# Attention and two mixture-of-experts layers on one core: the order of all instructions searched anew, with a tighter rule for taking operations and GpSimd's durations read from the trace

## The chip, the cores and the metric

The kernel runs on one core of one Trainium2 chip. The time is the device time of one execution in microseconds (us), the median over the runs of a kernel. The engines are called PE (TensorE, matrix multiplication), ACT (ScalarE), DVE (VectorE), POOL (GpSimd) and SP (SyncE, which here does nothing but issue DMAs). Each engine works through its own instructions strictly in the order in which the program lists them, and waits for the other engines by semaphores.

## The reference

Three layers for 4 batches, each with a sequence of 576 positions:

```python
# 1: attention, 8 heads of 64; 32 global positions see all, 512 local ones see the
#    global ones and a window of 32 to either side
s_g = scale * np.matmul(q_g, k_all.transpose(0, 1, 3, 2))
out_g = np.matmul(sm(s_g), v_all)
s_l = np.concatenate([s_lg, np.where(mask, s_ll, -1e9)], axis=-1)
out_l = np.matmul(sm(s_l), np.concatenate([v_g, v_l], axis=2))
# 2: causal attention by 4 experts, two of them taken for each position
logits = x @ w_gate
for e in range(E):
    q = x @ wq[e]; k = x @ wk[e]; v = x @ wv[e]
    ye = softmax(causal(scale * (q @ k.transpose(0, 2, 1)))) @ v @ wo[e]
    out += gate[e] * ye
# 3: wide layer with a convolution over 3 positions and a gate
h = np.maximum(x @ w_in, 0.0)
conv_out = sum(conv_w[k] * hp[:, k:k + S, :] for k in range(3))
out = h * (1.0 / (1.0 + np.exp(-conv_out))) @ w_out
```

## The kernel before, in words

**Stages.** For each batch b there are three stages. Stage A (`stage_a`, with `local` and `glob`) is layer 1: two halves u of the heads, each with two pairs of heads z. A pair's local scores (`scoresA`, L575 and L583) go to a tile of two PSUM banks; DVE takes the maxima (L586), POOL scales them (L372 on `st`), ACT makes eight exponentials (L592), PE transposes them in two groups of four (L599), ACT copies the transposes out of PSUM (L601), PE multiplies with the values (`pvA`, L612), DVE divides by the sums (L619 to L621), PE transposes the result (L629), and ACT and DVE split it into a high and a low part (L631, L378). The global rows of both pairs of a half take the same way in one piece (L648, L652, L654 and L656, L665, L667, then `pvG`, L675, and L679 to L699). Stage B (`stage_b`, `tiles`, `last`) is layer 2: projections (L727 for queries and keys, L747 for values and the gate), scores by query tiles (L811), a softmax whose exponentials are normalised on POOL (`nrmB`, L830), transposes (L838), products with the values (L857). The gate of a batch is a chain of small operations on DVE, POOL and ACT (L765 to L779). Stage C is layer 3: a product with `wo` and `w_in` multiplied beforehand (`h`, L940), the convolution (L372 on POOL, L955 on DVE), the gate (L959, L960), a split (L964, L378) and the product with `w_out` (`out`, L982), and a store (L998 and L1000, at the very end L989, L992 and L994). Matrices enter PE as a high and a low part, in three products each.

**Once only.** The weights `wqv` are loaded in four pieces and split (ACT L449, POOL L375). `wo` is loaded and split (ACT L495, DVE L378 on `wo`). `w_in` and `w_out` come in 8 pieces each and are decoded from 64-bit numbers (L477 to L487) and split; `w_in` is multiplied with `wo` (L514).

**What sets the order.** No order is written by hand. The functions record operations (`op`), each with an engine, a planned duration, and a priority; the class `Schedule` then lists all of them in one order by a planner that keeps a clock for each engine (`run`). A priority is a time on a line: the stage's begin and end from the table `PLAN`, a place inside it from `SUB`, and for each of the 1,906 operations a correction from the table `FINE`. At each step `run` looks at every engine's operations that are ready: those are allowed whose priority is at most `HORIZON` behind the least one that is still open; of the allowed ones that could begin within `SLACK` of the earliest, the one of least priority is taken, where for PE an operation in another tile mode than the last counts as `HOLD` later. Buffers (work tiles, PSUM banks, three `kq` tiles, four `v` tiles) are given out in the same pass; `CAPS` limits how many buffers of a kind may be held at a time. The loads of `kq`, `v` and the weights are operations of SP like all others, and each queue keeps the order of the list.

```python
            if o.prio > limit:
                continue
...
            c = min((c for c in cands if c[0] <= m + self.SLACK), key=rank)
```

PE's array works in several tile modes: whole (128x128: projections, `h`, `out`, all transposes), 64x32 (L575, L583, L648), 128x32 (L612, L675, L901), 64x128 (L811), 128x64 (L857). Ahead of all, nine matmuls with no use for the result keep PE busy until the first inputs are there (L1024).

Of the kernel before, what the change touches and what calls it, by code (L numbers as in the profile page):

```python
# [8 lines left out]
F32 = mybir.dt.float32  # L9
# [5 lines left out]
ALU = mybir.AluOpType  # L15
# [7 lines left out]
LEAST = 2.0 ** -15  # L23
MOST = 2.0 ** 125
# [121 lines left out]
class Schedule:  # L146
# [4 lines left out]
    SLACK = 0.092  # L151
    HOLD = 0.538
    HORIZON = 3714.57
# [153 lines left out]
def t_act(n, psum=False, ptr=0):  # L307
    return (167 + 0.83 * n + (0 if psum else 33) + 93 * ptr) * 1e-3


def t_dve(n, stt=False):
    return (150 + 1.04 * n + (70 if stt else 0)) * 1e-3


def t_pool(n, two=False):
    return (200 + (2.1 if two else 1.05) * n) * 1e-3


PLAN = {"A": [(-119.1, -47.3), (-21.7, 63.1), (38.1, 315.4), (307.0, 360.9)],
        "B": [(-137.7, -21.3), (148.2, 259.2), (249.9, 388.0), (376.3, 509.9)],  # L320
        "C": [(148.2, 401.7), (371.1, 480.9), (486.2, 654.7), (-670.0, 740.1)],
        "F": (162.2, -63.1),
        "U": (116.3, 210.9),
        "W": (-56.5, -20.9)}


CAPS = dict(raw=1, t=36, p=62, P=37, PT=2, PU=33, hb=44, cv=110, Pg=117, PGT=84)

MEM = (14, 11, 3, 4, 4)

SUB = {"lk": -1.365, "lv": -20.969, "ly": -0.281, "lw": -129.791, "ag": 0.056, "az": 0.113, "bq": -0.039, "bp": 0.366, "bv0": -1.297,
       "bv": 0.609, "bg": 2.203, "b0": -0.896, "b1": 1.269, "b2": 1.01, "b3": 1.37, "bl": 1.25, "bs": 0.036, "ch": 0.098,
       "co": 0.775, "cm": 0.686, "cf": -0.537, "cz": 0.902, "pi": 0.0, "pu": 0.0}


@with_exitstack
def body(ctx, tc, kq, vA, wqv, woT, w_in, conv_w, w_out, cmask, out, trace=None,
         tune=None):
    nc = tc.nc
    NB = kq.shape[0]  # L340
    pe, act, dve, pool, sp = nc.tensor, nc.scalar, nc.vector, nc.gpsimd, nc.sync

    sb = ctx.enter_context(tc.tile_pool(name="sb", bufs=1))
    ps = ctx.enter_context(tc.tile_pool(name="ps", bufs=1, space=PSUM))
# [20 lines left out]
    W = lambda n=1, keep=0, group=None: Buf(W_, n, keep, group)  # L365
# [3 lines left out]
    op = sch.op  # L369

    def scale_pool(dst, src, s):
        pool.tensor_scalar(dst, src, s, 1.0, op0=ALU.mult, op1=ALU.mult)  # L372
# [26 lines left out]
    vB = T([128, 5, 4, 65], F32, "vB")  # L399
# [55 lines left out]
    def decode(srcs, n, lead, tag, on_pool, spare=None):  # L455

        if spare:
            raw, t = Buf(D_, 1, 1), Buf(D_)
            p, tv, pv = (t, 1), (lambda: t.ap()[:, :512]), (lambda: t.ap()[:, 512:])
            dz = ["dz"]  # L460
# [635 lines left out]
```

## Time and profile before

| | before |
|---|---|
| median of 3 runs | 422.12 us (421.61 to 422.59) |
| the profiled execution, its own time | 423.22 us |
| its span, first to last instruction | 421.1 us |
| outside the span | 2.1 us |
| mean granted clock of PE | 0.986 |
| moved by DMA | 42.34 MB |

The span is what the profile shows in detail; the profiled execution is 1.1 us over the median of the runs. PE is busy nearly throughout, so the parts of the span that can shrink are those in which PE waits, those in which its clock is low, and what it loses between operations of different kinds.

### The profile page before, as it was taken

The page shows a single profiled execution, that of the slowest core. Times are in us where ns is not written, and L with a number is a line of the kernel's source. Part 1 is how long each engine was busy: PE and PEld are TensorE (multiplying, and loading weights), DVE is VectorE, ACT ScalarE, POOL GpSimd, SP SyncE. Part 2 cuts the span into 40 slices and gives each one's busy share as a digit, 9 for nine tenths or more (in the row PEclk, how much of TensorE's full clock was granted, in tenths as well). Part 3 has the DMA queues.
Part 4 walks back from the last instruction along what each step waited for, and adds up shares of the span by engine and source line. Part 5 has one row for each costly group of instructions (what it writes and reads, how often), then busy time and mean ns, then how long its engine had stood idle before and what let it go on. Part 6 is the DMA issues. An engine that isn't in the chain of part 4 may idle for free.

```text
span 421.1 us, 13314 instructions
## 1 busy us (share of the span) xinstructions
PE 402.0 (95%) x5605; PEld 362.5 (86%) x5605; DVE 281.5 (67%) x559; ACT 253.1 (60%) x616; POOL 172.7 (41%) x358
## 2 busy tenths in 40 slices
PE   7867899899899999999999999999999999999996
PEld 3656699677589999999889999899999999999996
DVE  2249858987787688886356558568675637758650
ACT  2866765765866746676476565675554556554531
POOL 3442563675775526460313232543331662262110
PEclk9888999999999999999999999999999999999999
DMA  8998922624523620233330200000000000000101
GB/s 309 396 345 299 339 98 75 215 90 147 184 82 107 207 97 2 89 125 125 120 127 0 94 5 2 28 29 2 2 2 2 26 28 29 29 0 28 54 26 54
DMA packets 15179, 42.34 MB, mean 101 GB/s; under 512 B 1552, under 2 KB 6416, under 8 KB 15120
## 3 DMA queue, kind: packets, MB, share of 16 engines
q1 hardware_dynamic: 15120, 41.49, 27.9%
q8 instruction: 44, 0.72, 0.7%
q14 instruction: 15, 0.12, 0.1%
HBM read 37.03 MB, written 4.46 MB: 99 GB/s over the span
## 4 chain that ended last, share of the span: by engine, by line
PE 84%; ACT 6%; DVE 4%; issue 3%; POOL 2%; DMA 1%; SPq 0%; ACTq 0%; DVEq 0%
PE acc L982 21%; PE acc L940 12%; PE acc L727 12%; PE acc L747 7%; PE acc L811 4%; PE acc L857 4%; PE acc L838 4%; PE acc L599 3%; PE acc L612 3%; PE acc L583 3%; ACT work L592 2%; PE acc L629 2%; DMA work<-in_w_out_dram 1%; PE acc L514 1%; PE acc L648 1%
## 5 line engine op out<-in xcount | busy, mean ns | idle before, releaser
L982 PE MATMUL acc<-xg,wuh 128*128 128x272 f32 x512 | 99.4, 292 | 0.0
L982 PEld LDWEIGHTS acc<-xg,wuh 128*128 128x128 f32 x512 | 79.9, 188 | 1.6 <-issue 1.2
L955 DVE SCALAR_TENSOR_TENSOR work<-work,cw 128x272 f32<-128x272 f32 x128 | 68.9, 560 | 18.2 <-POOL work L372 16.8
L982 PE MATMUL acc<-xg,wul 128*128 128x272 f32 x256 | 73.5, 287 | 0.0
L372 POOL TENSOR_SCALAR work<-work,cw 128x272 f32<-128x272 f32 x64 | 34.6, 551 | 53.3 <-ACT work L947 47.5
L940 PE MATMUL acc<-xg,wfh 128*128 128x274 f32 x256 | 51.6, 297 | 0.5 <-ACT work L667 0.5
L830 POOL TENSOR_SCALAR work<-work,st,gate 128x128 f32<-128x128 f32 (+3 forms) x64 | 46.5, 735 | 7.9 <-DVE st L827 6.1
L727 PE MATMUL acc<-xg,wqvh 128*128 128x272 f32 x256 | 49.7, 292 | 0.0
L982 PEld LDWEIGHTS acc<-xg,wul 128*128 128x128 f32 x256 | 48.2, 188 | 0.0
L592 ACT ACTIVATE work<-acc,st 128x128 f32<-128x128 f32 x128 | 37.1, 384 | 13.8 <-POOL st L372 13.7
L823 ACT ACTIVATE work<-acc,st 128x128 f32<-128x128 f32 (+3 forms) x64 | 33.1, 524 | 17.3 <-DVE st L816 12.0
L940 PEld LDWEIGHTS acc<-xg,wfh 128*128 128x128 f32 x256 | 40.2, 189 | 1.5 <-ACT work L667 0.8
L727 PEld LDWEIGHTS acc<-xg,wqvh 128*128 128x128 f32 x256 | 39.9, 188 | 0.9 <-issue 0.7
L940 PE MATMUL acc<-xg,wfl 128*128 128x274 f32 x128 | 37.1, 290 | 0.0
L727 PE MATMUL acc<-xg,wqvl 128*128 128x272 f32 x128 | 36.8, 287 | 0.0
L586 DVE TENSOR_REDUCE st<-acc 128x8 f32<-128x1024 f32 x16 | 19.5, 1219 | 22.6 <-PE acc L583 22.5
L947 ACT ACTIVATE work<-acc 128x546 f32<-128x546 f32 x32 | 20.0, 628 | 21.2 <-PE acc L940 17.6
L747 PE MATMUL acc<-wqvh,xg 128*128 128x260 f32 (+1 forms) x160 | 31.3, 286 | 0.0
L378 DVE TENSOR_TENSOR xg<-acc,xg 128x512 fp32r<-128x512 f32 (+3 forms) x56 | 22.6, 410 | 12.4 <-ACT xg L631 3.4
L840 ACT ACTIVATE work<-acc 128x512 f32<-128x512 f32 (+1 forms) x44 | 23.7, 558 | 11.3 <-PE acc L838 10.6
L378 DVE TENSOR_TENSOR xg<-work,xg 128x544 fp32r<-128x544 f32 x32 | 23.7, 744 | 9.4 <-ACT xg L964 8.6
L964 ACT ACTIVATE xg<-work 128x544 fp32r<-128x544 f32 x32 | 20.9, 659 | 13.8 <-DVE work L960 9.4
(138 smaller groups left out, 865.3 us busy)
## 6 DMA issues: line engine op xcount, KB each, us to landing
v<-in_vA_dram SPq DMA_DIRECT2D x32, 487.5 KB, 5.1
kq<-in_kq_dram SPq DMA_DIRECT2D x16, 624.0 KB, 5.2
work<-in_w_out_dram SPq DMA_DIRECT2D x8, 512.0 KB, 5.7
early<-in_w_in_dram SPq DMA_DIRECT2D x8, 512.0 KB, 6.8
out_dram<-work SPq DMA_DIRECT2D x15, 272.0 KB, 2.2
early<-in_wqv_dram SPq DMA_DIRECT2D x4, 386.0 KB, 8.8
early<-in_woT_dram SPq DMA_DIRECT2D x1, 512.0 KB, 9.0
out_dram<-work SPq DMA_DIRECT2D x2, 136.0 KB, 1.7
```

Source lines behind the costliest of these rows:

```text
L372: pool.tensor_scalar(dst, src, s, 1.0, op0=ALU.mult, op1=ALU.mult)
L378: dve.tensor_tensor(lo, src, hi.bitcast(F32), op=ALU.subtract)
L592: op("ACT", t_act(128, 1, 1), lambda y=y, t=t, sl=sl: act.activation(P[y].ap()[:, sl], S_(y)[:, sl], AF.Exp, bias=st.ap()[:, 8 + 4 * y + t ...
L727: pe.matmul(acc.ap()[:, 512 * z:512 * z + 272], wa[:, c, m], xa[:, s], start=(n == 0), stop=(n == 11))
L747: pe.matmul(acc.ap()[:r, :260], x[:, o_ + 128 * i:o_ + 128 * i + r], wa[:, c, :], start=(n == 0), stop=(n == 11))
L823: op("ACT", t_act(w, 1, 1) + .21, lambda tv=tv, st=st, y=y, k_=k_, Pb=Pb, c=c, h=h, w=w: act.activation(Pb.ap()[:, c:c + w], tv()[:, y, k_ ...
L830: op("POOL", t_pool(w), lambda Pb=Pb, st=st, c=c, h=h, e=e, w=w, i=i: pool.tensor_scalar(Pb.ap()[:, c:c + w], Pb.ap()[:, c:c + w], st.ap() ...
L840: op("ACT", t_act(128 * nb, 1), lambda PT=PT, tp=tp, nb=nb: act.activation(PT.ap()[:, :128 * nb], tp.ap()[:, :128 * nb], AF.Copy), r=[tp], ...
L940: pe.matmul(acc.ap()[:, 512 * f:512 * f + 274], a[:, p, sl], ov_(b)[:, x, p, 270 * z:270 * z + 274], start=(k == 0), stop=(k == 5))
L955: op("DVE", t_dve(272, 1), lambda hv=hv, cvv=cvv, f=f, F=F, z=z, k=k, o_=o_: dve.scalar_tensor_tensor(cvv()[:, f], hv()[:, f, o_:o_ + N], ...
L964: op("ACT", t_act(544), lambda G=G, cv=cv: act.activation(G.ap()[:, :544], cv.ap()[:, :544], AF.Copy), r=ct, w=[(G, 0)], tag="gh")
L982: pe.matmul(acc.ap()[:, 512 * m:512 * m + N], w[:, F, sl], G.ap()[:, o_ + N * f:o_ + N * f + N], start=(F == 0 and n == 0), stop=(F == 7 a ...
```

## The change

Only numbers change: three constants of the planner, the tables `FINE`, `PLAN`, `CAPS` and `SUB`, and the planned durations of some operations of POOL. The operations, their operands and the buffers' sizes stay. `HORIZON` falls from 3714.57 (no limit in practice) to 0.69, so that operations are taken nearly in the order of their priorities; `SLACK` is 0; `HOLD` is larger. `FINE` has other numbers throughout (its first entries are shown).

```diff
-    SLACK = 0.092
-    HOLD = 0.538
-    HORIZON = 3714.57
+    SLACK = 0.0
+    HOLD = 0.97
+    HORIZON = 0.69
...
-    FINE = {0: -42.4, 1: 62.9, 2: 79.2, 3: 48.2, 4: -51.1,
+    FINE = {0: -19.0, 1: 99.2, 2: 109.9, 3: 110.1, 4: 78.8,
...
-CAPS = dict(raw=1, t=36, p=62, P=37, PT=2, PU=33, hb=44, cv=110, Pg=117, PGT=84)
+CAPS = dict(raw=22, t=50, p=74, P=35, PT=13, PU=38, hb=19, cv=118, Pg=105, PGT=78)
...
-        op("POOL", 0.3, lambda: pool.memset(vB, 0.0), w=[("vB", i) for i in range(5)] + ["vBone", "vBraw"])
+        op("POOL", 1.2, lambda: pool.memset(vB, 0.0), w=[("vB", i) for i in range(5)] + ["vBone", "vBraw"])
...
-        op("POOL", t_pool(n), lambda: pool.tensor_scalar(a(F32), a(F32), MOST, LEAST, op0=ALU.min, op1=ALU.max), r=dz, w=[t], tag=tag)
+        op("POOL", t_pool(n) - .125, lambda: pool.tensor_scalar(a(F32), a(F32), MOST, LEAST, op0=ALU.min, op1=ALU.max), r=dz, w=[t], tag=tag)
...
-        op("POOL", .25, lambda: scale_pool(st.ap()[:, 8:16], st.ap()[:, 0:8], 0.125), r=[st], w=[(st, 1)], tag="sclA")
+        op("POOL", .205, lambda: scale_pool(st.ap()[:, 8:16], st.ap()[:, 0:8], 0.125), r=[st], w=[(st, 1)], tag="sclA")
...
-            op("POOL", .29, lambda i=i, r=r: pool.tensor_copy(lg[:r, i], vB[:r, i, :, 64]), r=[("vB", i)], w=[("lg", i)] + (["lg"] if i == 0 else []), tag="lg")
+            op("POOL", .19, lambda i=i, r=r: pool.tensor_copy(lg[:r, i], vB[:r, i, :, 64]), r=[("vB", i)], w=[("lg", i)] + (["lg"] if i == 0 else []), tag="lg")
...
-                    op("POOL", t_pool(w), lambda Pb=Pb, st=st, c=c, h=h, e=e, w=w, i=i: pool.tensor_scalar(
+                    op("POOL", .342 + .00084 * w, lambda Pb=Pb, st=st, c=c, h=h, e=e, w=w, i=i: pool.tensor_scalar(
```

The lists of instructions show what moves. PE, ACT, DVE, POOL and SP have the same operations as before; ACT and DVE have two instructions more each, because for one more half the small copies L699 and L378 fall into two pieces of 64x32. Counted over PE's list, the tile mode changes 124 times instead of 134; from the first projection (L747) on it is 108 instead of 113, and between whole-array products and transposes there are 90 changes instead of 86. Up to that first projection the list holds the same instructions of PE in both kernels, in another order. In the second half of the program the list is nearly the old one, block by block.

**PE, first half of the first batch.** L583 is the end of a `scoresA` (the third), the transposes of exponentials are L599, of the global ones L665, L612 is `pvA`, L675 `pvG`, L648 the global scores of the second half. Before:

```order
L583 MATMUL acc<-kq 32x128 x32
L599 MATMUL acc<-ident,work 128x128 x4
L675 MATMUL acc<-v,work 32x65 x20
L599 MATMUL acc<-ident,work 128x128 x4
L612 MATMUL acc<-v,work 32x65 x32
L684 MATMUL acc<-ident,work 128x128
L599 MATMUL acc<-ident,work 128x128 x8
L629 MATMUL acc<-ident,work 128x128 x4
L612 MATMUL acc<-v,work 32x65 x32
L648 MATMUL acc<-kq 32x480 x4
L648 MATMUL acc<-kq 32x64 x4
```

With the change:

```order
L583 MATMUL acc<-kq 32x128 x32
L599 MATMUL acc<-ident,work 128x128 x4
L665 MATMUL acc<-ident,work 128x128 x5
L599 MATMUL acc<-ident,work 128x128 x4
L612 MATMUL acc<-v,work 32x65 x32
L675 MATMUL acc<-v,work 32x65 x20
L599 MATMUL acc<-ident,work 128x128 x4
L648 MATMUL acc<-kq 32x480 x4
L648 MATMUL acc<-kq 32x64 x4
L684 MATMUL acc<-ident,work 128x128
L599 MATMUL acc<-ident,work 128x128 x8
L629 MATMUL acc<-ident,work 128x128 x4
```

All three first `scoresA` now stand ahead of the first transpose (before, transposes stood between them), the first `pvA` stands ahead of `pvG`, and the second half's global scores come before the second `pvA` and no longer behind it.

**SP, the first loads.** `kq` holds queries and keys of a pair of heads, `v` the values of one head (four of them per half), `wqv` and `woT` weights, `cmask` masks. Before:

```order
L427 DMA kq<-in_kq_dram 128x1248
L433 DMA cb<-in_cmask_dram 128x928
L427 DMA kq<-in_kq_dram 128x1248
L427 DMA v<-in_vA_dram 128x975
L427 DMA kq<-in_kq_dram 128x1248
L437 DMA cb<-in_cmask_dram 128x304
L427 DMA early<-in_wqv_dram 128x772
L427 DMA v<-in_vA_dram 128x975
L427 DMA early<-in_wqv_dram 128x772 x2
L427 DMA v<-in_vA_dram 128x975 x2
```

With the change:

```order
L433 DMA cb<-in_cmask_dram 128x928
L427 DMA kq<-in_kq_dram 128x1248 x2
L427 DMA early<-in_woT_dram 128x4x256
L427 DMA work<-in_conv_w_dram 128x48
L427 DMA kq<-in_kq_dram 128x1248
L427 DMA early<-in_wqv_dram 128x772
L427 DMA v<-in_vA_dram 128x975
L427 DMA early<-in_wqv_dram 128x772
L427 DMA v<-in_vA_dram 128x975
L427 DMA early<-in_wqv_dram 128x772
L427 DMA v<-in_vA_dram 128x975 x2
```

`woT` and the small `conv_w` are now ahead of all values; the small second piece of `cmask` has gone to a later place.

**POOL at the first gate.** The rows run from the first `epsB` (L826) to the scaling of the next batch's maxima (L372 on `st`); L767, L770 and L768 belong to the gate, L507 to the decoding of `w_in`. Before:

```order
L826 TENSOR_SCALAR st<-st 128x4
L767 TENSOR_TENSOR gw_84<-gw_84,cb 128x80
L770 TENSOR_TENSOR lg<-lg,gmx 128x20
L826 TENSOR_SCALAR st<-st 128x4
L768 TENSOR_TENSOR gw_83<-gw_83,gw_84 128x80
L372 TENSOR_SCALAR st<-st 128x8
```

With the change:

```order
L826 TENSOR_SCALAR st<-st 128x4
L767 TENSOR_TENSOR gw_84<-gw_84,cb 128x80
L770 TENSOR_TENSOR lg<-lg,gmx 128x20
L507 TENSOR_TENSOR early<-early,xg 128x512
L768 TENSOR_TENSOR gw_83<-gw_83,gw_84 128x80
L372 TENSOR_SCALAR st<-st 128x8
```

An L507 has come between L770 and L768, and the second L826 has gone behind the scaling.

## Rows read from the trace of the kernel before

**Rows 1.** The page: busy time, and PE, DVE, clock, DMA in 40 slices.

```profile
PE 402.0 (95%) x5605; PEld 362.5 (86%) x5605; DVE 281.5 (67%) x559; ACT 253.1 (60%) x616; POOL 172.7 (41%) x358
...
PEclk9888999999999999999999999999999999999999
DMA  8998922624523620233330200000000000000101
```

**Rows 2.** Busy time by stage: window, its length, PE, PEld, DVE, ACT, POOL, PEclk, DMA share, GB/s.

```profile
0.00:49.40 49.40, 36.88 (x893) 25.70 (x893) 26.61 (x52) 31.77 (x81) 20.45 (x39) 0.90 0.92 333
49.40:120.00 70.60, 67.62 (x1014) 56.60 (x1016) 56.22 (x119) 47.51 (x124) 41.89 (x71) 1.00 0.43 151
120.00:240.00 120.00, 120.00 (x1871) 111.68 (x1862) 83.53 (x160) 76.98 (x195) 50.04 (x102) 1.00 0.27 89
240.00:401.30 161.30, 160.93 (x1716) 152.23 (x1713) 109.76 (x220) 91.84 (x208) 58.82 (x146) 1.00 0.06 23
```

**Rows 3.** The chain that ended last, pieces between 18 and 50 us.

```profile
18.72 0.78 PE acc L675 x40
19.50 0.59 PE acc L599 x4
20.09 0.82 PE acc L612 x48
20.90 2.96 issue
23.86 0.66 PE acc L612 x16
...
34.39 1.64 issue
...
44.63 1.05 PE acc L648 x16
...
47.22 1.45 issue
```

**Rows 4.** Windows up to each of four stops of PE; the counts matter.

```profile
0.00:16.10 16.10, 12.83 (x223) 7.31 (x223) 3.49 (x4) 6.85 (x16) 5.48 (x17) 0.89 0.91 342
0.00:22.00 22.00, 16.52 (x350) 9.98 (x351) 5.39 (x8) 12.75 (x34) 8.52 (x21) 0.92 0.95 355
0.00:35.50 35.50, 25.72 (x606) 17.05 (x606) 14.02 (x27) 21.76 (x57) 13.57 (x30) 0.90 0.96 354
0.00:48.20 48.20, 36.14 (x859) 25.13 (x859) 26.23 (x51) 31.20 (x80) 19.38 (x37) 0.89 0.92 333
```

**Rows 5.** Timeline of PE, the first stop, and of SP, the third and fourth `v`.

```profile
16.19 0.67 PE L583 MATMUL acc<-kq 64*32 64x128 f32 x31 [0.24 <-issue]
...
7.59 1.56 SPq L427 DMA_DIRECT2D v<-in_vA_dram  x2
```

**Rows 6.** DMA issues between 8.5 and 9.3 us: the fourth `v`, us to landing.

```profile
v<-in_vA_dram SPq DMA_DIRECT2D x1, 487.5 KB, 9.1
```

**Rows 7.** Windows of ten us in the start.

```profile
10.00:20.00 10.00, 8.45 (x205) 6.14 (x205) 2.74 (x4) 8.46 (x26) 4.29 (x6) 0.83 1.05 398
30.00:40.00 10.00, 7.77 (x237) 6.26 (x225) 9.74 (x16) 6.25 (x18) 3.26 (x8) 0.88 0.94 367
40.00:50.00 10.00, 7.79 (x214) 5.75 (x214) 8.72 (x21) 8.03 (x20) 4.93 (x6) 0.95 0.82 252
```

**Rows 8.** Timeline of DVE between 24.5 and 31 us.

```profile
25.00 0.69 DVE L621 TENSOR_TENSOR work<-acc,st 128x512 f32<-128x512 f32 x1
...
25.80 1.21 DVE L378 TENSOR_TENSOR wo<-early,wo 128x1024 fp32r<-128x1024 f32 x1
27.04 0.30 DVE L378 TENSOR_TENSOR xg<-acc,xg 64x32 fp32r<-64x32 f32 x2
...
30.55 0.72 DVE L652 TENSOR_REDUCE st<-acc 128x1 f32<-128x544 f32 x1
```

**Rows 9.** The chain between 321 and 327 us.

```profile
321.00 0.92 PE acc L811 x12
321.91 1.70 PE acc L982 x12
323.61 1.52 PE acc L940 x12
325.13 1.49 PE acc L982 x12
```

**Rows 10.** The chain at the end of a wait for POOL, 269 us; two groups of POOL's instructions.

```profile
269.23 3.35 POOL work L830 x6
...
L830 POOL TENSOR_SCALAR work<-work,st,gate 128x128 f32<-128x128 f32 x16 | 10.4, 656 | 0.2
L507 POOL TENSOR_TENSOR early<-early,xg 128x512 f32<-128x512 f32 x8 | 10.8, 1345 | 8.3 <-DVE st L619 4.7 <-ACT xg L506 3.5
```

More of the change, by code (lines that the diff above doesn't have):

```diff
@@ L316, in t_pool @@
     return (200 + (2.1 if two else 1.05) * n) * 1e-3
[L319 to L324, printed above, removed]
-CAPS = dict(raw=1, t=36, p=62, P=37, PT=2, PU=33, hb=44, cv=110, Pg=117, PGT=84)
+PLAN = {"A": [(-119.7, -48.2), (-21.9, 62.9), (38.1, 315.6), (307.4, 361.3)],
+        "B": [(-137.7, -21.3), (148.5, 259.4), (249.8, 388.0), (376.1, 509.8)],
+        "C": [(148.5, 401.8), (371.4, 481.1), (486.1, 655.3), (-668.3, 746.0)],
+        "F": (162.3, -62.8),
+        "U": (116.1, 210.9),
+        "W": (-52.9, -24.7)}
+CAPS = dict(raw=22, t=50, p=74, P=35, PT=13, PU=38, hb=19, cv=118, Pg=105, PGT=78)
 MEM = (14, 11, 3, 4, 4)
-SUB = {"lk": -1.365, "lv": -20.969, "ly": -0.281, "lw": -129.791, "ag": 0.056, "az": 0.113, "bq": -0.039, "bp": 0.366, "bv0": -1.297,
-       "bv": 0.609, "bg": 2.203, "b0": -0.896, "b1": 1.269, "b2": 1.01, "b3": 1.37, "bl": 1.25, "bs": 0.036, "ch": 0.098,
-       "co": 0.775, "cm": 0.686, "cf": -0.537, "cz": 0.902, "pi": 0.0, "pu": 0.0}
+SUB = {"lk": 0.237, "lv": -18.39, "ly": -0.48, "lw": -130.134, "ag": 0.055, "az": 0.113, "bq": -0.04, "bp": 0.368, "bv0": -1.295,
+       "bv": 0.609, "bg": 2.204, "b0": -0.896, "b1": 0.535, "b2": 1.01, "b3": 1.37, "bl": 1.249, "bs": 0.036, "ch": 0.098,
+       "co": 0.775, "cm": 0.684, "cf": -0.537, "cz": 0.902, "pi": 0.0, "pu": 0.0}
 @with_exitstack
@@ L652, in glob @@
         op("DVE", t_dve(544), lambda: dve.tensor_reduce(st.ap()[:, 0:1], G.ap()[:, 32:576], axis=AX.X, op=ALU.max, negate=True), r=[G], w=[st], tag="maxG")
-        op("POOL", .25, lambda: scale_pool(st.ap()[:, 1:2], st.ap()[:, 0:1], 0.125), r=[st], w=[(st, 1)], tag="sclG")
+        op("POOL", .19, lambda: scale_pool(st.ap()[:, 1:2], st.ap()[:, 0:1], 0.125), r=[st], w=[(st, 1)], tag="sclG")
         op("ACT", t_act(480, 1, 1), lambda: act.activation(Pg.ap()[:, :640].rearrange("p (n c) -> p n c", n=5)[:, :, 32:128],
@@ L829, in tiles @@
                     Pb, c, h, e = Ps[n // per], w * (n % per), y * np_ + k_, 2 * p + y
-                    op("POOL", t_pool(w), lambda Pb=Pb, st=st, c=c, h=h, e=e, w=w, i=i: pool.tensor_scalar(Pb.ap()[:, c:c + w], Pb.ap()[:, c:c + w], st.ap()[:, 12 + h:13 + h], gate[:, i, e:e + 1],
+                    op("POOL", .342 + .00084 * w, lambda Pb=Pb, st=st, c=c, h=h, e=e, w=w, i=i: pool.tensor_scalar(Pb.ap()[:, c:c + w], Pb.ap()[:, c:c + w], st.ap()[:, 12 + h:13 + h], gate[:, i, e:e + 1],
                        op0=ALU.mult, op1=ALU.mult), r=[(st, 4), gt], w=[(Pb, n % per)], tag="nrmB")
```

2 lines of the change are left out of this document (1 added, 1 removed).

## The prediction

> **What bounds the kernel now.** I read the page's busy times first, then the windows by stage, then the chain of waits in the start, then single rows. PE is busy for 402.0 us and no other engine for over 281.5 [rows 1]; the reader should see in the slices that the clock is below full only in the first five, the same slices in which the DMA queues are full. The windows by stage say where the 19 us without PE lie [rows 2]: in the start, up to the first projection at 49.4 us, PE works 36.88 of 49.40 us, so 12.5 us are lost, at a mean clock of 0.90; from there to 120 us 3.0 us are lost; from 120 to 401.3 us only 0.4 us. The rest is the warm-up's begin and the tail after the last product. So from 120 us on a new order can win nothing by filling gaps, only by fewer changes of mode, and whatever gain there is must come from the start, with a little from the stretch behind it.
>
> In the start the chain shows three kinds of loss. First, stops of PE for which no engine is to blame ("issue"): 2.96 us at 20.90, 1.64 at 34.39, 1.45 at 47.22 [rows 3] and 0.24 at 15.9 [rows 5], 6.3 us together. The matmuls begun by these four stops are 223, 350, 606 and 859 [rows 4]: the steps are 127, 256 and 253, once and twice about 127 each, and each matmul has its weight load, so a step is 254 or 255 instructions. A stop that comes by count belongs to the fetching of PE's own instructions, and a new order of the same instructions meets it at the same counts. Second, waits for the DMA and ACT: PE's first product with values starts at 18.72 [rows 3], and the fourth `v` tile, without which it can't run, was issued as the second of two from 7.59 us on, at about 8.8 [rows 5], and landed 9.1 us later [rows 6], at 17.9. Third, from 30 us on DVE is nearly full, 9.74 and 8.72 of 10 us [rows 7].
>
> **The change part by part.** The tables and constants act only through the order; the work stays, so each term is a difference of waiting.
>
> *Start, up to the stop at matmul 350.* Before, matmul 350 lies in `pvA`: `pvG` from 18.72, four transposes, 48 of 64 matmuls, stop at 20.90. Now `pvA` needs just the first two `v` tiles and goes ahead; `pvG` follows, and counting the list, matmul 350 is the 32nd of its 40. Ahead of and with the fourth `v`, the old queue holds three `kq`, two pieces of masks, three `wqv` and four `v`, 5,288 KB; the new one has 512 KB of `woT` and 24 KB of `conv_w` in addition and the 76 KB mask less, 5,748 KB. The 460 KB more take 1.16 us at 398 GB/s [rows 7], so the fourth `v` lands at about 19.1. From there 32 of 40 matmuls of a `pvG` that lasts 0.78 us take 0.6 us: the stop comes at about 19.8 and no longer at 20.90. **Term: -1.1 us.** ACT must not be later than that; its list has the `woT` split (L495) put in early, but all three score products now come one behind the other, so its exponentials are never short of work, where it worked 8.46 of 10 us from 10 to 20 us [rows 7].
>
> *Start, after that stop.* The stop itself I leave at 2.96 us. Behind it, the normalising of the first `pvA` (0.69 us and two short operations, [rows 8]) is now done before it, and in its place 16 matmuls of the global scores, 1.05 us [rows 3], stand ahead of the second `pvA`: about a us won, about a us given back. The global maximum (L652, 0.72 us) and the split of `woT` on DVE (1.21 us, [rows 8]) now stand earlier on DVE, ahead of the stretch in which it is full up to the first projection; I take 0.4 us for that, between 0 (DVE waits at that stretch's head for later data anyway) and 1.9 (both come off). **Term: -0.4 us.** Bounds for the whole start: the 12.5 us less the four stops leave 6.2 us, more than that can't go; on the other side, if each of the three shorter stops grew to the longest seen, 2.96, it would cost 2.72, 1.32 and 1.51, or 5.5 us.
>
> *Changes of mode.* The chain shows the same 12 products of L982 taking 1.70 us behind a block in another mode and 1.49 behind L940 in the same one [rows 9], 0.2 us for a change out and back. From the first projection on the list has 5 changes fewer; the 4 more between products and transposes are dearer than nothing and cheaper than that. **Term: -0.4 us**, between -0.5 and 0. The Trainium skill, TensorEngine Tiling (Array Packing), section Key Properties, says that changing the tiling mode drains TensorE; the rows agree that a change costs something, and their 0.2 us is the price used.
>
> *From 49 to 120 us, and single gaps behind.* 3.4 us are lost in PE's gaps [rows 2]. One of the longest waits is for six normalisations on POOL in a row, 3.35 us [rows 10]; their planned duration was 0.200 + 0.00105 x 128 = 0.33 us for 128 columns and is 0.342 + 0.00084 x 128 = 0.45 now, against 656 ns measured [rows 10], so the new order leaves more room for them. **Term: -0.5 us.** Its bounds are -3.4 (every gap goes) and +1.0: at the first gate an L507, 1,345 ns [rows 10], now stands before L768 and the scaling on which the next exponentials and their transposes hang, and if the gate's second comparison (L766) didn't come earlier on DVE to make up for it, that row would go straight into PE's next gap.
>
> *The tail* ends with the same instructions and the same store; 0. The two more small copies on ACT and DVE are hidden, since neither engine sets the end there; uncovered they would cost what two of them take now, 0.30 us [rows 8].
>
> Sum: 1.1 + 0.4 + 0.4 + 0.5 = 2.4 us. Against the profiled execution's own 423.22 us this is 420.8; that execution was 1.1 us over the median, so the median comes to 422.12 - 2.4 = **419.7 us**, 0.6% faster. About 0.2%, 0.84 us, is what a measurement of this kernel can tell from no change.
>
> **The rivals.**
>
> *A, more comes off.* The stops at fixed counts are not bound to the order, or PE's remaining waits in the start go with the earlier `pvA`. About 5 us would go: 417.1. For it speaks that PE's four stops differ so much (0.24 to 2.96), that is, something hides most of the first one; against it, that three of them are long. The Trainium skill, Runtime: NRT & Kernel Launch, section Instruction fetch mechanics, has the cost of crossing an instruction block as mostly hidden; by that rule the 6.3 us would be an accident of this order. The trace does not agree here: its longest stop at such a count is 2.96 us.
>
> *B, the start's gain stays in the start.* DVE is full from 30 to 50 us and near 8 of 10 us up to 120 [rows 2, 7], so an earlier `pvA` may only make PE wait longer for DVE; then the 1.5 us of the start and the 0.5 behind it come back as waits, and the changes of mode alone remain: 421.7, no difference that can be told.
>
> *C, slower: the stops grow.* Their place is the start, at matmuls 223, 606 and 859. With the score products one behind another PE now runs through its list faster up to 223 (before, it reached it after waits for ACT, and stopped 0.24 us [rows 5]), so less time is left in which instructions come in, under the same full queues. If that stop takes 2.96 and the one at 606 too, 2.72 + 1.32 = 4.0 us are lost against 2.4 won: 423.7. This decides from the point where the four stops sum to more than 6.3 + 2.4 = 8.7 us; what speaks against it is that PE is ahead of ACT there, so that part of a longer first stop would be waiting anyway.
>
> *D, the durations are not what the trace said.* If POOL's operations last longer next to other neighbours than planned, the change does not do what it says, and the middle term goes: 420.2. For it: 656 ns against the new formula's 450 [rows 10], so the new numbers are still the short ones. The Trainium skill, SBUF — State Buffer, section Who interferes with whom, says of the port pair that DVE and GpSimd share that issue order decides who blocks; a duration would then depend on the order that it helped to find. No run here shows which of the two blocked.
>
> **How the numbers follow.** The forecast 0.40, A 0.13, B 0.19, C 0.18, D 0.10. The forecast, A and D are faster by over 0.2%: 0.63; B is within it: 0.19; C is slower: 0.18. The range reaches from A's time, 417.1, rounded down a little for its bound, to the lower half of C: 417.0 to 423.4; inside lie the forecast, B and D with 0.69 and about 0.13 of A and C. The forecast's own range is 418.5 to 421.0.
>
> **What would show it.** Right: the first projection (L747) starts at 47.5 to 48.5 us and not at 49.5; `pvA` stands before `pvG` in the timeline, with a stop of 2 to 3 us inside `pvG` that begins near 20 us; windows up to the stops again count about 223, 350, 606 and 859; PE's busy time from the first projection on is 0.3 to 0.5 us less. Wrong: an equal or later first projection with DVE still full behind it (B), stops that sum to over 8.7 us (C), or stops at other counts or none (A). A gap of a us before the transposes at 79 us behind a late scaling would say that POOL's order at the gate costs what it must.

## The result, and the profile after

The changed kernel takes 415.45 us (median of 4 executions, 413.78 to 417.05) against 421.93 us of the kernel before on the same chip (4 executions): ratio 0.9844, 95% interval 0.9801 to 0.9887, 6.5 us less. The forecast was 419.7 us with a range down to 417.0. Beside the experiments the kernel before ran 51 times more, median 421.89 us; the changed one ran 10 times in all, median 416.52 us, 5.4 us less. These executions come from several chips. A ratio in this document is always one to the kernel before on the same chip. The profiled execution is one of the quicker: 414.91 us, span 412.8, mean granted clock 0.996.

The page after, beside [rows 1]: PE busy, clock and DMA in 40 slices.

```profile
PE 394.9 (96%) x5605; PEld 358.5 (87%) x5605; DVE 273.4 (66%) x561; ACT 250.1 (61%) x618; POOL 175.1 (42%) x358
...
PEclk9989999999999999999999999999999999999999
DMA  8998533635603520235430200100000000000011
```

PE works 7.1 us less on the same 5,605 matmuls (part of that is the clock of these two executions, experiment 4). The clock's digit is 8 in one slice only; before it was 8 in three, the second to the fourth, and not in the first five as the prediction reads them. The same windows as in [rows 2]:

```profile
0.00:49.40 49.40, 36.62 (x931) 26.58 (x932) 28.59 (x57) 34.50 (x91) 22.97 (x42) 0.97 0.90 339
49.40:120.00 70.60, 68.91 (x1064) 58.08 (x1065) 56.67 (x124) 48.21 (x127) 44.11 (x74) 1.00 0.42 147
120.00:240.00 120.00, 119.91 (x1849) 111.90 (x1827) 78.22 (x160) 75.61 (x200) 43.97 (x96) 1.00 0.30 97
240.00:401.30 161.30, 161.30 (x1724) 153.96 (x1723) 109.62 (x221) 90.48 (x201) 64.04 (x147) 1.00 0.06 19
```

38 matmuls more are begun by 49.4 us, and the idle time from there to 120 us is 1.7 us where it was 3.0. The chain in the start, beside [rows 3]:

```profile
9.52 9.58 DMA v<-in_vA_dram
...
19.14 0.66 PE acc L675 x32
19.80 1.81 issue
21.61 0.45 PE acc L675 x8
...
26.62 1.08 PE acc L612 x64
...
38.73 0.35 issue
...
44.72 3.16 PE acc L747 x24
```

The fourth `v` lands at 19.10 and the stop at matmul 350 begins at 19.80, both as forecast (19.1 and 19.8). But the stop lasts 1.81 us and not 2.96, there is none at 606 in this execution, and the first projection (L747) starts at 44.72 where it started at 49.44. Windows that end in a stop, beside [rows 4], and the first stop beside [rows 5]:

```profile
0.00:13.80 13.80, 8.43 (x223) 4.50 (x224) 3.50 (x4) 6.88 (x16) 3.74 (x15) 1.00 0.88 327
0.00:21.50 21.50, 12.37 (x350) 7.70 (x351) 6.22 (x8) 13.38 (x34) 9.35 (x21) 1.00 0.93 357
0.00:39.00 39.00, 26.72 (x733) 18.13 (x733) 19.52 (x38) 26.19 (x68) 17.16 (x33) 0.96 0.94 359
```

```profile
13.87 0.59 PE L583 MATMUL acc<-kq 64*32 64x128 f32 x18 [1.03 <-issue]
```

The counts are 223 and 350 again, and 733, which is 127 more than 606. The stops sum to 1.03 + 1.81 + 0.35 = 3.2 us against 6.3.

The start and everything behind the first projection, before and then after:

```profile
0.00:49.44 49.44, 36.92 (x894) 25.70 (x894) 26.61 (x52) 31.77 (x81) 20.49 (x39) 0.90 0.92 333
49.44:417.60 368.16, 364.81 (x4713) 336.80 (x4712) 254.60 (x506) 221.02 (x534) 152.22 (x320) 1.00 0.20 70
```

```profile
0.00:44.72 44.72, 31.95 (x893) 21.91 (x893) 24.79 (x52) 30.71 (x79) 20.69 (x37) 0.96 0.93 350
44.72:409.30 364.58, 362.79 (x4712) 336.60 (x4712) 248.31 (x509) 219.11 (x539) 154.39 (x322) 1.00 0.21 72
```

So in this pair of profiles 4.7 us come off the start and 3.6 us off the rest, of which 1.55 us are idle time (368.16 - 364.81 = 3.35, now 1.79) and 2.0 us are PE's own time for the same products. The forecast had 1.5 and 0.9. One pair of profiles is not enough for the first of these numbers, as experiment 4 shows.

**Where the stops come from.** The trace of DMA shows transfers of 16,384 bytes on a queue of their own, 44 in a run, about one for every 127 matmuls. What one of them brings is called a block of PE's instructions here. This is one of them among the data, 19.0 to 20.5 us of the changed kernel:

```profile
DMA packets 173, 0.60 MB, mean 399 GB/s; under 512 B 16, under 2 KB 16, under 8 KB 172
...
q1 hardware_dynamic: 172, 0.58, 98.8%
q8 instruction: 1, 0.02, 4.3%
```

Each stop ends 1.34 to 1.54 us after the end of such a transfer:

| stop at matmul | transfer, us | PE goes on, us | later by |
|---|---|---|---|
| before, 223 | 13.71 to 14.74 | 16.19 | 1.45 |
| before, 350 | 21.36 to 22.43 | 23.86 | 1.43 |
| before, 606 | 33.42 to 34.50 | 36.03 | 1.53 |
| before, 859 | 46.34 to 47.33 | 48.67 | 1.34 |
| after, 223 | 11.28 to 12.33 | 13.87 | 1.54 |
| after, 350 | 19.18 to 20.21 | 21.61 | 1.40 |
| after, 733 | 36.60 to 37.63 | 39.08 | 1.45 |

In the start, with two to eight loads in flight, the transfer for a block starts 1.4 to 5.3 us after PE has gone on with the block ahead of it, in both kernels. Behind the start, where mostly no load or one is in flight, it starts between some 2.5 us before PE's array begins that block and 1.4 us after. The order of events that fits is: a block is begun, the next one is asked for, and the request waits behind data. No record shows the request itself; experiments 2 and 3 put this to the test. By it a stop is what is left of the delay when PE has run through its block, and a late entry into one block makes the next one late.

### The profile page after: what moved, and what is told of

Read it like the earlier page. It is cut to its first block, busy times and chain, and to the rows that moved or that the text cites. A ratio compares the mean times of both kernels' runs of the same rounds, so it can differ in the third digit from the quotient of the medians.

```text
span 412.8 us, 13305 instructions
## 1 busy us (share of the span) xinstructions
PE 394.9 (96%) x5605; PEld 358.5 (87%) x5605; DVE 273.4 (66%) x561; ACT 250.1 (61%) x618; POOL 175.1 (42%) x358
## 4 chain that ended last, share of the span: by engine, by line
PE 88%; DMA 4%; ACT 3%; DVE 2%; issue 1%; SPq 0%; POOL 0%; ACTq 0%; DVEq 0%
PE acc L982 23%; PE acc L727 12%; PE acc L940 12%; PE acc L747 7%; PE acc L857 5%; PE acc L811 4%; PE acc L838 4%; PE acc L612 4%; PE acc L599 3%; PE acc L583 3%; PE acc L514 3%; DMA v<-in_vA_dram 2%; PE acc L648 2%; DMA early<-in_woT_dram 2%; PE acc L629 1%
## 5 line engine op out<-in xcount | busy, mean ns | idle before, releaser
L982 PE MATMUL acc<-xg,wuh 128*128 128x272 f32 x512 | 99.4, 292 | 0.1
L982 PEld LDWEIGHTS acc<-xg,wuh 128*128 128x128 f32 x512 | 80.0, 188 | 1.3 <-issue 0.6
L982 PE MATMUL acc<-xg,wul 128*128 128x272 f32 x256 | 73.6, 287 | 0.0
L955 DVE SCALAR_TENSOR_TENSOR work<-work,cw 128x272 f32<-128x272 f32 x128 | 64.1, 525 | 13.8 <-POOL work L372 12.8
L372 POOL TENSOR_SCALAR work<-work,cw 128x272 f32<-128x272 f32 x64 | 36.6, 580 | 51.6 <-ACT work L947 28.6
L830 POOL TENSOR_SCALAR work<-work,st,gate 128x128 f32<-128x128 f32 (+3 forms) x64 | 45.4, 718 | 11.2 <-DVE st L827 9.3
L982 PEld LDWEIGHTS acc<-xg,wul 128*128 128x128 f32 x256 | 48.2, 188 | 0.0
L378 DVE TENSOR_TENSOR xg<-acc,xg 128x512 fp32r<-128x512 f32 (+3 forms) x58 | 22.7, 401 | 18.6 <-ACT xg L699 6.5
L960 DVE SCALAR_TENSOR_TENSOR work<-work 128x544 f32<-128x544 f32 x32 | 23.7, 742 | 12.1 <-ACT work L959 12.0
L747 PE MATMUL acc<-wqvh,xg 128*128 128x260 f32 (+1 forms) x160 | 31.5, 286 | 0.2 <-DVE xg L378 0.2
L378 DVE TENSOR_TENSOR xg<-work,xg 128x544 fp32r<-128x544 f32 x32 | 24.5, 769 | 6.4 <-ACT xg L964 6.4
```

The source lines that it names most:

```text
L378: dve.tensor_tensor(lo, src, hi.bitcast(F32), op=ALU.subtract)
L747: pe.matmul(acc.ap()[:r, :260], x[:, o_ + 128 * i:o_ + 128 * i + r], wa[:, c, :], start=(n == 0), stop=(n == 11))
L830: op("POOL", .342 + .00084 * w, lambda Pb=Pb, st=st, c=c, h=h, e=e, w=w, i=i: pool.tensor_scalar(Pb.ap()[:, c:c + w], Pb.ap()[:, c:c + w], ...
L955: op("DVE", t_dve(272, 1), lambda hv=hv, cvv=cvv, f=f, F=F, z=z, k=k, o_=o_: dve.scalar_tensor_tensor(cvv()[:, f], hv()[:, f, o_:o_ + N], ...
L960: op("DVE", t_dve(544), lambda hv=hv, cvv=cvv, z=z: dve.scalar_tensor_tensor(cvv(), cvv(), 1.0, hv()[:, :, 1:1 + N], op0=ALU.add, op1=ALU. ...
L982: pe.matmul(acc.ap()[:, 512 * m:512 * m + N], w[:, F, sl], G.ap()[:, o_ + N * f:o_ + N * f + N], start=(F == 0 and n == 0), stop=(F == 7 a ...
```

## Experiments

Each experiment ran beside the kernel before, on one of three chips: experiments 1 and 3 and the first of 2 on one where it had a median of 421.8 us (24 executions), experiment 4, the second of 2 and the first of 6 on another (422.87, 16 executions), experiment 5 and the second of 6 on a third (421.46, 11).

**1. Half of the order each.** The planner's choice is replaced by a given list: up to the first projection that of one kernel, behind it that of the other.

```diff
...
-            t, o, places = pick
+        for n in self.LIST:
+            o = self.ops[n]
...
```

New start, old rest:

> The list of the changed kernel up to its first projection, the old list for all the rest. If the start gives most of the gain (first projection at 44.7 us and no longer at 49.5), this kernel takes 421.9 - 4.7 = 417.2 us, between 416 and 418.5, with the first projection at 44.2 to 45.7. Rival: the new order is worth its gain only as a whole, because the old rest waits for VectorE and for loads that the new start leaves for later; then the 4.7 us come back as gaps between 49 and 120 us and it takes 420 to 422.

419.45 us (10 executions), ratio 0.9944 (0.991 to 0.9978), by neither answer. The ten executions fall into two groups, five from 417.5 to 418.3 us and five from 420.6 to 421.5, and the median lies in the empty space between; the profile below is of the quicker group. What parts the groups is not known: a mean clock of 0.988 and one of 0.996 occur in both.

Old start, new rest:

> The old list up to its first projection, the new list for all the rest. If the two parts add up, it takes 421.9 - (6.5 - 4.7) = 420.1 us, between 419 and 421, with the first projection at 49 to 50 us and about 1.5 us less of gaps of PE behind it. Rival: the gaps behind the start were shorter only because VectorE came out of the new start ahead; then it takes 421.5 to 422.5.

419.90 us (10 executions), ratio 0.9955 (0.9923 to 0.9987), as expected; but its first projection comes at 47.90, earlier than expected, and its gaps hardly shrink. Windows of the two, new start first:

```profile
0.00:43.71 43.71, 32.65 (x893) 23.15 (x894) 26.42 (x52) 30.85 (x79) 19.51 (x36) 0.96 0.93 354
43.71:412.00 368.29, 364.90 (x4712) 336.82 (x4712) 257.35 (x507) 222.42 (x537) 155.50 (x323) 1.00 0.21 73
```

```profile
0.00:47.90 47.90, 33.33 (x894) 22.57 (x894) 26.41 (x53) 31.67 (x80) 19.73 (x37) 0.96 0.93 342
47.90:414.20 366.30, 363.20 (x4712) 336.63 (x4712) 247.92 (x509) 218.68 (x538) 155.14 (x322) 1.00 0.21 70
```

The new start is worth 2.35 us by the medians (4 us in the quicker group, about 1 in the other), and the rest behind it stays as it was (368.29 against 368.16). The new rest alone is worth 1.9 us by the medians and by its window (366.30), nearly all of it in PE's own time (363.20); its idle time stays at 3.1. Only both together bring the idle time down to 1.79. So about half of the gain lies behind the start, where the forecast had seen little.

**2. Other counts, the same order.** 24 warm-up matmuls of 64 columns more move each count 24 matmuls earlier in the program.

```diff
+        for k in range(24):
+            pe.matmul(P_.view(7, 1)[:, :64], wz.bitcast(BF)[:, :128], wz.bitcast(BF)[:, 128:192], start=True, stop=True)
```

> The changed kernel with 24 more matmuls of 64 columns in the warm-up, which nobody reads. If PE's stops come by the count of its instructions, they stay at matmuls 222 and 350 by count, which is 24 matmuls earlier in the program: the first after about 22 of the 64 matmuls L583 of the third local scores (now 46), the second after 8 of the 40 of L675 (now 32). Rival: the stops belong to places (to a wait that the records don't name); then they stay behind 46 and 32 matmuls. The time tells little: 414 to 417 by either.

415.13 us (4 executions), ratio 0.9863 (0.9817 to 0.9909). The stops did not move to the same counts as expected: at 222 and 350 there was none, since PE now entered the first block before it waited for `kq`, so that the transfers came at 10.38 and 16.50 us and no longer at 11.28 and 19.18. The others kept to their counts (478, 606, 733, 860), that is, 24 matmuls earlier in the program, so the stops go by count and not by place:

```profile
30.96 0.64 PE L583 MATMUL acc<-kq 64*32 64x128 f32 x25 [1.06 <-issue]
...
253.04 0.40 PE L583 MATMUL acc<-kq 64*32 64x128 f32 x2 [1.00 <-issue]
```

The first projection came at 43.51, 1.2 us earlier, but 1.0 us was lost again at 252 us with the DMA queues nearly empty: there a block holds nothing but short matmuls, PE runs through its 127 in 2.3 us (249.76 to 252.04; the expectations below say 2.0), and the next block, whose transfer runs from 250.33 to 251.50, takes longer to come. Two things keep this from showing that the addition helps this order. By the ratios, 0.9863 against 0.9844 and 0.9859, it wins nothing. And two of the four profiles of the same start without the addition have no stop at 223 or 350 either, with transfers at 10.6 to 10.7 and 16.9 to 17.1 us and the first projection at 43.71 (experiments 1 and 5).

The same addition to the kernel before:

> The kernel before with 24 more warm-up matmuls of 64 columns, nothing of its order changed. Theory: its instructions come late because PE asks for a block only when it enters the one before; with the shift it enters the first one about 1.5 us earlier, ahead of its first wait for kq, so the block for matmul 350 comes about 2 us earlier, that stop shrinks from 2.96 to 0.5 to 2, and the time falls by 1 to 3 us, to 419 to 421. Rival: what ends the start is the data, and a shorter stop turns into a wait for them: 421.4 and over.

420.37 us (11 executions), ratio 0.9942 (0.992 to 0.9964), 2.5 us less with not one operation reordered, as the theory said. All three profiles of this start without the addition have stops at 223 and 350, and both are gone here, where the transfers come at 9.62 and 17.26 us and no longer at 13.71 and 21.36. Of the four stops, 5.3 and 6.3 us in the two profiles of the kernel before, this is left:

```profile
32.73 0.64 PE L583 MATMUL acc<-kq 64*32 64x128 f32 x25 [0.54 <-issue]
```

The first projection comes at 46.55 us (49.44 and 48.34 before). Some of the 2.5 us is PE's clock: by the count of experiment 4 these executions have 1.7 stretches at half clock on average, those of the kernel before on the same chip 2.75. At one, two and three stretches each the difference is 1.2, 1.6 and 2.2 us.

**3. More data ahead of the instructions.** Three transfers of 624 KB, for nothing, behind the eighth `v`.

```diff
+    scr = nc.dram_tensor("scr", (4, 128, KB + S), F32, kind="Internal").ap()
...
             o.fn()
+            if o.n == 73:
+                for k in range(3):
+                    sp.dma_start(scr[k], kq[k, 0])
```

> The changed kernel with three more transfers of 624 KB, from DRAM to DRAM and read by nobody, issued on SP right behind the eighth v load (at 28 us). If the length of PE's stops is set by how long the packet with its instructions waits behind data in the DMA queues, the packet that starts at 30.6 us now starts 1.5 to 4 us later and PE stops for 1 to 4 us at matmul 604 (33 us), where it does not stop now, and the first projection comes 2 to 4 us later: 417 to 420 us. Rival: the fetch does not depend on the data; then that packet still starts at about 30.6, there is no stop at matmul 604, and only loads that come late (kq for the second batch, used at 40 us) may cost up to 2 us.

418.25 us (9 executions), ratio 0.9919 (0.9891 to 0.9947): 1.7 us over the changed kernel's 416.52, and 2.5 to 3.2 us by the ratios, for transfers that no instruction waits for. The transfer for matmul 606 starts at 32.45 us and no longer at 30.60, and where the first profile of the changed kernel had no stop there is now this row (the lines are one further on in this kernel):

```profile
35.10 0.37 PE L584 MATMUL acc<-kq 64*32 64x128 f32 x1 [2.71 <-issue]
```

The stop at this count differs between executions without the additional data too: the four profiles of the same start have none, 0.48, 1.62 and, in experiment 1, this one:

```profile
31.62 0.27 PE L583 MATMUL acc<-kq 64*32 64x128 f32 x1 [1.61 <-issue]
```

Counted from PE's entry into the block ahead, the transfer starts 5.5 us later here (26.91 to 32.45) and 2.3, 2.8, 3.7 and 3.9 us later in those four. So one profile shows the delay 1.6 us longer than the longest without the data, and the stop 1.1 us longer.

**4. The same kernels again, and the clock.** Unedited.

> The changed kernel again, unedited, for more executions and a second profile. The first profile of it has PE's clock at half in one stretch (21.7 to 25 us), that of the kernel before in three (10.4, 24.0 and 37.8 us), each beginning after PE had stood still or nearly so. Theory: part of the 8.3 us between the two profiled spans is this, and the number of such stretches differs from execution to execution of the same kernel; then the executions here fall into groups by granted clock, about 1 us apart per stretch, around a median of 415 to 416.5, and the second profile may have two. Rival: the stretches belong to the order; then every execution of it has the mean clock 0.996 of the first. The stops by count (223, 350, 733) come again at these counts under both; their lengths may move by a us.

417.38 us (6 executions), ratio 0.9859 (0.983 to 0.9888), a little slower than the theory had it. The second profile has stops at 350 (2.04 us) and 606 (0.48) and none at 223 or 733, so the expectation that the same three come again failed: the counts at which a stop can come are fixed within one or two matmuls, but which of them shows one, and how long, differs between executions of one kernel.

> The kernel before again, for a second profile. Stops of PE at 223, 350, 606 and 859 matmuls and at no others; if the number of half-clock stretches is not bound to the order, one or two here instead of three and a span 1 to 2 us shorter; if it is bound, three again.

One execution, 421.92 us; stops at 223, 350, 606 and 859 (1.19, 2.69, 0.79 and 0.66 us), its span 1.3 us shorter and its mean clock 0.992, which counts two stretches, all as the theory said. PE's clock, in windows around each stretch at half clock of the first pair, before:

```profile
10.00:14.00 4.00, 3.72 (x77) 2.78 (x78) 0.00 (x0) 3.14 (x9) 0.77 (x1) 0.57 1.05 414
23.90:27.40 3.50, 3.50 (x29) 3.01 (x28) 2.69 (x8) 1.88 (x6) 0.26 (x1) 0.51 0.96 331
37.60:41.20 3.60, 3.30 (x17) 2.78 (x15) 3.46 (x8) 1.86 (x5) 0.77 (x2) 0.53 0.49 196
```

The first profile after:

```profile
11.00:15.00 4.00, 2.24 (x77) 1.73 (x77) 0.65 (x2) 3.04 (x8) 0.20 (x1) 1.00 1.03 397
21.60:25.10 3.50, 3.49 (x29) 1.66 (x29) 1.18 (x4) 0.85 (x1) 1.96 (x2) 0.54 1.02 414
37.60:41.20 3.60, 3.25 (x124) 2.18 (x122) 3.60 (x11) 3.15 (x9) 0.80 (x1) 1.00 0.65 201
```

The second profile of the same kernel:

```profile
11.00:15.00 4.00, 3.26 (x75) 2.46 (x75) 0.50 (x1) 2.90 (x8) 0.00 (x0) 0.58 1.01 396
21.60:25.10 3.50, 3.21 (x28) 1.49 (x27) 1.18 (x4) 0.85 (x1) 1.96 (x2) 0.54 1.03 418
38.80:42.30 3.50, 3.50 (x104) 3.17 (x108) 2.88 (x6) 3.39 (x10) 0.47 (x1) 0.52 0.48 152
```

So one order has one such stretch in one execution and three in another. Each follows on PE standing still: in the kernel before it stood for 1.54 us until 10.28, 2.96 until 23.86 and 1.64 until 36.03; in the changed kernel for 1.81 until 21.61 in the first execution, and for 2.58 until 11.74, 2.04 until 21.89 and 2.11 until 38.73 in the second. Not every stop of that length has one behind it: the first execution of the changed kernel stood for 1.79 us until 11.74 at full clock after it. The window from 10 to 14 us has a mean clock of 0.57, so its stretch takes away 0.43 x 4.00 = 1.7 us of full clock, which lets the stretches of every execution be counted from its mean clock times its span:

The three groups with the most executions:

| stretches | before, mean us (executions) | after |
|---|---|---|
| 1 | 420.9 (11) | 414.4 (3) |
| 2 | 421.7 (19) | 416.6 (4) |
| 3 | 422.9 (15) | 417.4 (2) |

A line through all executions rises by 0.96 us per stretch before (51) and by 0.90 after (10). The mean number is 2.25 before and 2.2 after, so by this count the clock is no part of the gain. It is not the whole of the spread: the 11 executions before with one stretch lie between 418.9 and 422.5 us. And the first pair of profiles, three stretches against one, shows about 1.9 us of difference that the orders do not have.

What the start of each order takes, from all profiles with neither more warm-up matmuls nor more data (stops that came by count, in us):

| start, profile | stretches | at 223 | at 350 | at 606 | at 733 | at 859 | sum | first projection, us |
|---|---|---|---|---|---|---|---|---|
| old, before | 3 | 0.24 | 2.96 | 1.64 | 0 | 1.45 | 6.3 | 49.44 |
| old, before again | 2 | 1.19 | 2.69 | 0.79 | 0 | 0.66 | 5.3 | 48.34 |
| old, with the new rest | 1 | 1.18 | 1.71 | 1.04 | 0 | 0 | 3.9 | 47.90 |
| new, after | 1 | 1.03 | 1.81 | 0 | 0.35 | 0 | 3.2 | 44.72 |
| new, after again | 3 | 0 | 2.04 | 0.48 | 0 | 0 | 2.5 | 47.09 |
| new, with the old rest | 1 | 0 | 0 | 1.61 | 0.90 | 0 | 2.5 | 43.71 |
| new, experiment 5 | 2 | 0 | 0 | 1.62 | 0 | 0 | 1.6 | 43.71 |

The new start is quicker in each of the four than the old one in any of the three, on average by 3.7 us, and its stops are 2.7 us less.

**5. GpSimd's old durations in the new tables.** The six changed durations only, `t_pool` back.

```diff
...
-                    op("POOL", .342 + .00084 * w, lambda Pb=Pb, st=st, c=c, h=h, e=e, w=w, i=i: pool.tensor_scalar(
+                    op("POOL", t_pool(w), lambda Pb=Pb, st=st, c=c, h=h, e=e, w=w, i=i: pool.tensor_scalar(
...
```

> The changed kernel with the old planned durations of GpSimd's operations and everything else new. The order that comes out differs from the changed kernel's in 31 rows on PE, 18 on DVE and 19 on ACT, all behind the first projection and most near the output projection. Theory: with operations taken nearly in the order of their priorities the durations hardly act when the list is made; the time is that of the changed kernel, 415.4 to 417.4. Rival: the durations are what sets POOL's operations early enough; then the gaps of PE behind the first projection (2.0 us in the changed kernel, 3.4 before) come back and the time is 417.5 to 419.

417.65 us (6 executions), ratio 0.9897 (0.9867 to 0.9927), a little above what the theory allowed. The interval overlaps with that of the changed kernel beside experiment 4 (0.983 to 0.9888), so by the time alone the two are not told apart. The start, whose order is the changed kernel's, had only one stop (1.62 us at 606) in its profile; behind the first projection:

```profile
43.71:409.10 365.39, 362.69 (x4712) 336.79 (x4712) 248.67 (x508) 219.30 (x539) 153.69 (x323) 1.00 0.21 72
...
80.88 0.66 PE L838 MATMUL acc<-ident,work 128*128 128x128 f32 x4 [0.74 <-ACT work L840]
```

Idle time is 2.70 us, 0.9 more than in the changed kernel, and most of that is the row shown, which the changed kernel does not have: there four of these transposes stand ahead of `pvA` and the others behind it. PE's own time is the changed kernel's (362.69 against 362.79 us), as the theory had it. That the 0.9 us of idle time depend on the durations is likely but not shown: three profiles of the changed order, with that of experiment 3, have 1.76 to 1.80 us against 2.70 in this single one, but the same wait stands in the profile of the old start with the new rest, where PE's list behind the first projection is the changed kernel's:

```profile
85.13 0.66 PE L838 MATMUL acc<-ident,work 128*128 128x128 f32 x4 [0.75 <-ACT work L840]
```

**6. Sixteen more warm-up matmuls.** The changed kernel with 16 more warm-up matmuls: the first count lies before the wait for `kq`, and the block at 252 us gets a longer run. The edit is that of experiment 2 with 16 for 24.

> The changed kernel with 16 more warm-up matmuls of 64 columns, so that the counts at which PE needs its next instructions lie 16 matmuls earlier in the program. 24 more took away the stops at 222 and 350 and brought the first projection forward by 1.2 us, and lost 1.0 us again at 252 us, where the block of instructions after a boundary held only short matmuls, which ran in 2.0 us. With 16 the boundary near 252 us falls where that block runs 2.9 us. Theory: no stop at 222, first projection at 43.4 to 44.4, a stop near 252 us of at most 0.5; time 414.0 to 415.2. Rival: the position of the boundaries is worth nothing over many executions: 415.5 and over.

414.98 us (5 executions), ratio 0.9813 (0.9788 to 0.9838); no stop at 222 or 350, 0.36 us near 254, the first projection at 44.63, a little late. Once more:

> The changed kernel with 16 more warm-up matmuls once more, as the version that beats both kernels so far: 414.98 median of 5 executions, all with one half-clock stretch. Theory: no stop at 222 or 350 and therefore one stretch, rarely two; median 414.5 to 415.5, at least 1 us under the changed kernel's 416.5 (10 executions). Rival: the five executions were lucky in the clock: 416 and over.

414.53 us (6 executions), ratio 0.9841 (0.9818 to 0.9864). Over the 11 executions the median is 414.58 against 416.52 of the changed kernel. Ten of the 11 have one stretch at half clock and one has three, so about one of these two microseconds is the clock. Against the changed kernel's own ratios, 0.9844 and 0.9859, the intervals overlap; that it is the quicker one rests on both series together. Even then it may win only through the clock: at one stretch each it has 414.6 us (10 executions) against 414.4 (3).

## Why the prediction was wrong

**"Start, up to the stop at matmul 350 ... Term: -1.1 us."** Right, in mechanism and size: 19.80 against 20.90, through the landing at 19.10 that the bytes ahead of the fourth `v` gave.

**"The stop itself I leave at 2.96 us"** failed. A stop has no length of its own. PE enters the block ahead earlier (13.87 where it was 16.19), so the next transfer ends 2.2 us earlier, while PE reaches matmul 350 only 1.1 us earlier, and 1.81 us are left of 2.96. In the other profiles of the new start 2.04, 0 and 0 are left. The three other stops, which the sum kept as they were, went from 3.3 us to 1.4 in the first pair. Where 1.1 + 0.4 was forecast for the start, the medians give 2.35 us (experiment 1, between two groups) and the profiles 3.7 on average. The first pair shows 4.7, of which about 1.9 is the clock. My forecast had no term for the clock, although [rows 2, 7] show it at 0.83 to 0.95 in the start; on average over executions it needed none.

What I overlooked stands in the kernel. The planner, whose code for this is the same in both kernels, counts PE's instructions, asks for a block about when the one ahead is begun, adds to its arrival what the loads in flight still have to move (`dma`), and adds the wait that is left (`stall`) to the planned time:

```python
                while count + o.size > page:
...
                    stall = max(0.0, fetched - at)
...
                    ask = max(fetched, at + stall - self.AHEAD * span / o.size)
                    fetched = ask + self.FETCH + self.BEHIND * min(1.6, max(0.0, dma - ask) * self.RATE * 1e-6)
```

So an order with shorter stops has a shorter planned time, and tables searched for that would shorten them, where the forecast took their lengths as given. No run takes this part out of the planner, so how much of the gain comes from it is not shown.

**"Changes of mode ... Term: -0.4 us, between -0.5 and 0"** failed as the whole account of PE's own time behind the first projection, which fell by 2.0 us, and by 1.6 with the new rest alone. For the changes themselves its size was about right. Worked out from the starts of the matmuls in the two traces, without idle time, the steps across a change of tile mode there, by the tile sizes in the records, are 116 before and 110 after and sum to 24.2 and 22.8 us. Such a step holds a matmul's own time as well: the 4,595 steps within a mode take 340.6 us before, 0.074 each. What a change adds to that is 0.13 us on average, 15.6 us in all before and 14.7 after. With the ordinary step taken line by line and by its operands it is 0.14 each, 16.1 and 15.8 us in all. The 0.2 us from [rows 9] is the step from L811 into L982, one change and not one out and back as I had it. So between 0.3 and 0.9 of the 2.0 us are the changes, and 1.1 to 1.7 us lie elsewhere in PE's steps, for which the forecast had nothing. What that is stays open.

**"From 49 to 120 us, and single gaps behind ... Term: -0.5 us."** Right in sign and inside its bounds, short in size: idle time behind the first projection fell by 1.55 us. About 0.9 of it went in the one profile with the old durations (experiment 5), so the reason given for the term may hold, but that is not shown; and the place was another: not the wait of 3.35 us for POOL, of which PE felt 0.2, but transposes near 81 us. The feared cost at the first gate did not show: the wait at the transposes there is 0.7 us, 0.6 before. In sum the first pair of profiles has 3.6 us behind the start against 0.9 forecast; by the medians of 5.4 us in all, this is the larger part of the miss.

**The rivals.** A was the nearest in size and half right in reason: the counts stay, the lengths do not, and at some counts there is no stop. The rule cited beside it (the Trainium skill, Runtime: NRT & Kernel Launch, section Instruction fetch mechanics) also says that an engine's sequencer fetches the next page by a DMA queue of its own while it executes the current one. The transfers are on such a queue and start about when the block ahead is begun, as that would have it, and they show when its "mostly hidden" fails: 1.4 to 5.3 us of delay where data fill the queues. B is excluded by the whole time, C by the stops' sum, 3.2 and not over 8.7. D, at 420.2 us, is excluded by the time; what the durations were worth is not settled (experiment 5). The middle term that it would take away came out larger, not at nothing.

## What to carry to other kernels

A stop by instruction count is, as far as these runs show, the end of a chain: block entered, next block asked for, queued behind the data in flight, landed, and 1.3 to 1.5 us later PE goes on. Cost a new order by when it enters each block, and try a few idle instructions ahead of everything before reordering anything: here 24 of them gave the old order 2.5 us, part of it through the clock, and nothing that can be told to the new one. Read what the planner counts before costing what it plans. And compare one profile with one profile only after counting the stretches at half clock in each; take differences of a few microseconds from stretches of the program without such noise, here the 368 us behind the first projection: 368.1, 367.9, 368.3 and 368.1 in four profiles of the old list, 364.5 and 364.6 in two of the new one. Even these depend on what stands ahead: behind the old start the new list takes 366.2.

## What the runs showed of the hardware that was not expected

Instructions wait behind data: three transfers of 624 KB that nobody needed cost 1.7 us, and the place where this shows first is a transfer of PE's instructions (loads behind them came later too, and the two are not told apart). Even with nearly idle queues a block of short matmuls that lasts 2.3 us stopped PE for 1.0 us, in one profile.

DVE needs 8.1 us less for its work in another order, 281.5 and 273.4 us, and the rest of the list decides it (254.60 and 257.35 us behind the first projection with the old one, 248.31 and 247.92 with the new one). Over half of it is one group, before and then after:

```profile
L955 DVE SCALAR_TENSOR_TENSOR work<-work,cw 128x272 f32<-128x272 f32 x128 | 68.9, 560 | 18.2 <-POOL work L372 16.8
```

```profile
L955 DVE SCALAR_TENSOR_TENSOR work<-work,cw 128x272 f32<-128x272 f32 x128 | 64.1, 525 | 13.8 <-POOL work L372 12.8
```

POOL's L372 beside it took 551 ns on average and now takes 580. The Trainium skill, SBUF — State Buffer, section Who interferes with whom, has DVE with two inputs in SBUF contend with a GpSimd instruction that reads there; the two means move in opposite senses, as that would have it, but no run here takes the overlap away, so it is not shown. It cost the kernel nothing either way, since DVE does not set the end.
